# Backward attention loop: the loads of a head put one by one between the DMA transposes, in a fixed order of the SP queue, and the stores moved a few units later

## Chip, cores, metric

One core of a Trainium2 chip. The metric is the device time of one execution in microseconds (us). SP is the engine that issues most DMAs; PE does matmuls, ACT the exponentials, DVE the products, POOL some additions. "Issue" is the time that an engine's sequencer spends on starting a DMA; the transfer itself runs on 16 DMA engines.

## The reference, cut to what matters

The reference is a transformer block (layer norm with modulation, attention with 32 heads of 16, squared-ReLU MLP) and the gradients of its inputs by `jax.vjp`; n = 2048 tokens, D = 512. The part at issue is the gradient of attention:

```
scores = jnp.einsum('bhqd,bhkd->bhqk', q, k) * Dh ** (-0.5)
p = _softmax(scores, axis=-1)
o = jnp.einsum('bhqk,bhkd->bhqd', p, v)
```

From the incoming gradient dO the kernel forms dS = P * (dO v' - row sum) and from it dK, dV and dQ.

## The kernel before

The backward loop handles 4 heads at a time (a "head group", here also just "head"; 8 in all) and in each 64 units of 128 queries x 512 keys. For a unit PE computes the scores and dO v', ACT the exponentials `E_u`, DVE the product `dS_u`, and SP issues a DMA that transposes `dS_u` (128 x 2048 bf16, 512 KB) from SBUF to SBUF, because dQ needs it with keys on the partitions. PE's `dqacc` reads the result 4 units later. PE, ACT and DVE follow the program's order (`manual_schedule`); the order of SP's DMAs is chosen by the recording layer's scheduler.

```python
def load_rows(dst, srcT, hg, cols, aux=None):
    for h in range(4):
        i = hg * 4 + h
        SP.dma_start(out=dst[32 * h:32 * h + DH, :], in_=srcT[i * DH:(i + 1) * DH, cols])            # 16 rows, 64 KB
        if aux is not None:
            SP.dma_start(out=dst[32 * h + DH:32 * h + DH + 1, :], in_=aux[i:i + 1, cols])            # 1 row, 4 KB
# ... (cut)
def load_kvq(hg):
    hs = hsets[hg % 2]                                   # two sets of k, q, v, do, qs
    load_rows(hs["k"], qkT_st[1], hg, slice(0, n))
    load_rows(hs["q"], qkT_st[0], hg, slice(0, n), m_st)
    load_rows(hs["v"], vT_st, hg, slice(0, n))
    ACT.dma_start(out=hs["qs"][:], in_=q_st[hg])
# ... (cut)
def transpose_unit(u):
    hg, kc, qc, qi = units[u]
    if qi == 0:
        dqt[u // 4] = tpool.tile([P, 4, 16, P], BF, name="dsT", tag="dsT")       # 2 buffers
    SP.dma_start(out=dqt[u // 4][:, qi], in_=bst[u][1].rearrange("p h k -> p (h k)"), transpose=True)
# ... (cut)
with tc.manual_schedule(engines={PE.engine, ACT.engine, DVE.engine}):
    for j in range(2 * NU + 10):                         # two steps j for each unit
        # ... load_head of the next head at unit 8; score; dp_pair; transpose_unit; k_quad, v_quad; dq_quad (cut)
```

A head's load is 24 "row loads" (16 of 64 KB for k, q, v and do, 8 of one row) and one load `qs` of 256 KB. At a head's end two results of 512 KB are stored (`dVKtP`, `dQtP`).

## Time and profile before

| | before |
|---|---|
| median, lowest and highest of the first 3 runs | 3083.7 us (3079.6 to 3087.5) |
| backward loop, first to last `dS_u` | 1423.4 to 2891.4 us, 1468.1 us |
| a head (heads 1 to 6) | 182.4 to 184.3 us |
| its 8 blocks of 8 units (head 1) | 25.9, 30.6, 20.6, 22.3, 20.5, 20.8, 21.7, 21.9 us |

The first view is the table by stretches: for the first 25 us of head 1, the next 31 us, and the rest of the head, how long each engine was busy, the granted PE clock, the busy share of the DMA engines and the rate. (Shares above 1 occur as packets overlap.)

```profile
core 0: us, PE busy (x) PEld busy (x) DVE busy (x) ACT busy (x) POOL busy (x), PEclk, DMA share, GB/s
1613.00:1638.00 25.00, 19.48 (x157) 5.06 (x154) 17.66 (x17) 16.82 (x34) 1.38 (x2) 0.78 1.09 218
1638.00:1669.00 31.00, 20.69 (x164) 5.52 (x163) 18.86 (x17) 17.66 (x36) 2.77 (x1) 0.78 0.94 181
1669.00:1797.00 128.00, 113.83 (x963) 32.53 (x960) 111.52 (x97) 104.28 (x208) 13.54 (x11) 0.90 1.16 198
```

In the third stretch everything is busy, DVE 111.52 of 128 us, and DMA over 1. In the second, at the shares of the third PE would have worked 28 us and DVE 27 of the 31; they did 7 to 8 us less, and DMA is below 1.

The next view is SP's timeline at the same place. Columns: start, length, line and operation, destination and source, count; L799 is the transpose, L112 a load of 16 rows, L114 of one row.

```profile
1632.06 1.97 SPq L799 DMA_TRANSPOSE dsT<-dS_u  x1
1634.08 0.99 SPq L112 DMA_DIRECT2D ik_11035<-qkT_st  x1
1635.16 5.70 SPq L799 DMA_TRANSPOSE dsT<-dS_u  x2
1640.91 0.57 SPq L112 DMA_DIRECT2D ik_11035<-qkT_st  x1
1641.53 0.41 SPq L112 DMA_DIRECT2D iq_11037<-qkT_st  x1
1641.99 0.28 SPq L114 DMA_DIRECT2D iq_11037<-m_st  x1
...
1648.73 0.28 SPq L114 DMA_DIRECT2D ido_11038<-d_st  x1
1649.11 8.35 SPq L799 DMA_TRANSPOSE dsT<-dS_u  x3
```

One k load stands alone (1634.08), then two transposes follow, and then 21 loads from 1640.91 to 1649.01, each 0.27 to 0.6 us of issue. For these 8 us SP issues no transpose. DVE's timeline shows the price, in brackets the idle time and who ended it:

```profile
1655.33 1.23 DVE L793 TENSOR_TENSOR dS_u<-psD_u,E_u 128x1024 bf16<-128x1024 f32 x1 [9.53 <-PE psD_u L791]
```

In the middle of a head, SP does nothing but transposes, 13 of them in 34.62 us, 2.66 us each:

```profile
1667.21 34.62 SPq L799 DMA_TRANSPOSE dsT<-dS_u  x13
```

The list of waits (who waited for whom: us in total, times, longest) and the lines of the chain of waits (share of the span):

```profile
DVE dS_u L793 <- PE psD_u L791: 205.8, 122, 10.7
PE dqacc L834 <- DMA dsT<-dS_u: 137.3, 79, 10.5
```

```profile
DMA dsT<-dS_u 14%; ACT ET L569 12%; PE psS_u L779 7%; PE dqacc L834 5%; ACT E_u L781 5%; PE accVK L816 3%; DVE dS_u L793 3%; PE accVK L807 3%; PE psST L567 2%; PE psS_x L779 2%; PE pm L410 2%; DMA dwp<-dw_st 2%; PE pm L430 1%; PE pm L492 1%
```

DVE's longest wait is 10.7 us, a stall like the one above; the entry `DMA dsT<-dS_u 14%` is the largest in the chain.

Which engine sets the pace? I counted the 256 B packets in the trace, 2048 for each transpose. The first packet of a transpose starts on average 0.01 us after the last of the previous one. So the DMA engines go from transpose to transpose without rest, and the loop is the sum of 511 intervals between the ends of neighbouring transposes, sorted here by what SP issued between the two:

```
before: between the transposes    count   interval us (mean)   from last packet to first packet
nothing                            467       2.66 (median 2.50)     0.01
one 64 KB k load                    19       3.38                   0.37
21 row loads                         7      11.01                   8.41
store dVKtP / dQtP                6 / 7      4.15 / 4.21            1.25 / 1.35
```

(Five more intervals, with reloads of gradients for the next stage, are left out here.)

A run of 21 loads costs 11.01 - 2.66 = 8.35 us, three single k loads 3 x 0.72 = 2.2 us: 10.5 us for the row loads of a head, 7 times. (The last of the 7 had only one k load alone, so there are 19 and not 21.)

### The profile page before, as it was taken

Reading aid. Unit: us, or ns where it says so; the run is one execution under the profiler, and the core shown is the slowest. Engines: PE = TensorE matmul, PEld = TensorE weight load, DVE = VectorE, ACT = ScalarE, POOL = GpSimd, SP = SyncE. Lnnn points to the kernel's source line nnn. Section 1 sums busy time; section 2 is a strip of 40 time slices with the busy share of each in tenths; the row PEclk is TensorE's granted clock in tenths of the full one; section 3 lists DMA queues with packets and bytes.
Section 4 is the critical chain, followed back from the end, with each engine's and each line's share of the span. In section 5 each row is a group of like instructions: output and inputs, shape, how many; then the busy total and the mean of one; then the engine's idle time right before and its main releaser. Section 6 shows DMA issues by size and latency. Waiting matters only on the chain.

```text
span 3082.2 us, 46295 instructions
## 1 busy us (share of the span) xinstructions
PE 2460.6 (80%) x17006; PEld 721.4 (23%) x17006; DVE 1785.3 (58%) x2165; ACT 2176.8 (71%) x3415; POOL 519.8 (17%) x487
## 2 busy tenths in 40 slices
PE   6799888688858885546887878878787887988878
PEld 2111122222212221222222222222222222222323
DVE  6000234333423442456787878878787887878783
ACT  4799989698859884103786868778686886877621
POOL 2110012211231224122010110101011010101151
PEclk9555589879986998777788978889798987888888
DMA  9741132724492359677999999999999999999941
GB/s 258 180 130 28 34 69 85 184 59 92 95 152 55 85 112 140 129 151 204 196 197 194 201 193 198 205 191 198 193 201 193 198 205 193 196 211 200 210 112 45
DMA packets 1403811, 475.54 MB, mean 154 GB/s; under 512 B 1321456, under 2 KB 1372660, under 8 KB 1403456
## 3 DMA queue, kind: packets, MB, share of 16 engines
q1 hardware_dynamic: 1390048, 445.31, 74.4%
q0 software_dynamic: 12384, 25.17, 5.0%
q8 instruction: 134, 2.20, 0.3%
q10 hardware_dynamic: 1152, 2.10, 0.3%
q14 instruction: 93, 0.76, 0.1%
HBM read 74.86 MB, written 70.54 MB: 47 GB/s over the span
## 4 chain that ended last, share of the span: by engine, by line
PE 32%; DMA 21%; ACT 17%; issue 11%; DVE 9%; SPq 3%; POOL 3%; DVEq 0%; POOLq 0%; ACTq 0%
DMA dsT<-dS_u 14%; ACT ET L569 12%; PE psS_u L779 7%; PE dqacc L834 5%; ACT E_u L781 5%; PE accVK L816 3%; DVE dS_u L793 3%; PE accVK L807 3%; PE psST L567 2%; PE psS_x L779 2%; PE pm L410 2%; DMA dwp<-dw_st 2%; PE pm L430 1%; PE pm L492 1%; DMA dw_st<-dwp 1%
## 5 line engine op out<-in xcount | busy, mean ns | idle before, releaser
L793 DVE TENSOR_TENSOR dS_u<-psD_u,E_u 128x1024 bf16<-128x1024 f32 x1024 | 1188.2, 1218 | 283.5 <-PE psD_u L791 205.8
L781 ACT ACTIVATE E_u<-psS_u 128x512 bf16<-128x512 f32 x1536 | 867.5, 635 | 316.0 <-PE psD_u L791 304.2
L569 ACT ACTIVATE ET<-psST 128x1024 bf16<-128x1024 f32 x1024 | 952.3, 1249 | 158.7 <-PE psST L567 157.9
L834 PE MATMUL dqacc<-dsT,KS_tok 128*32 128x512 bf16 x2048 | 210.9, 499 | 194.6 <-DMA dsT<-dS_u 137.3
L781 ACT ACTIVATE E_u<-psS_x 128x512 bf16<-128x512 f32 x512 | 334.8, 654 | 10.2 <-PE psD_u L791 9.3
L779 PE MATMUL psS_u<-ik_11035,iq_11037 32*128 32x512 bf16 x768 | 260.2, 435 | 8.8 <-DVE prows L712 3.4
L779 PE MATMUL psS_u<-ik_12082,iq_12084 32*128 32x512 bf16 x768 | 255.0, 425 | 3.9
L583 PE MATMUL oacc<-ET,vaug 128*32 128x512 bf16 x2048 | 253.8, 486 | 1.3 <-DVE ostage L587 1.3
L791 PE MATMUL psD_u<-iv_11036,ido_11038 32*128 32x512 bf16 x1024 | 225.2, 433 | 14.1 <-DVE dS_u L793 10.8
L849 POOL TENSOR_TENSOR dQacc<-dQacc,dqtmp 128x512 f32<-128x512 f32 x64 | 81.1, 1267 | 895.2 <-ACT dqtmp L844 895.2
L567 PE MATMUL psST<-qt_sb_107,kt_sb_105 32*128 32x512 bf16 x1024 | 203.4, 480 | 33.6 <-ACT ET L569 10.9
L791 PE MATMUL psD_u<-iv_12083,ido_12085 32*128 32x512 bf16 x1024 | 219.4, 422 | 6.7 <-DVE dS_u L793 3.9
L816 PE MATMUL accVK<-E_u,dOs_tok 128*16 128x512 bf16 x2048 | 224.6, 428 | 0.0
L567 PE MATMUL psST<-qt_sb_108,kt_sb_106 32*128 32x512 bf16 x1024 | 195.1, 477 | 27.1 <-ACT ET L569 14.3
L338 DVE COPY dwp<-pm 128x512 f32<-128x512 f32 (+1 forms) x102 | 67.3, 660 | 229.7 <-DMA dw_st<-dwp 152.3
L587 DVE COPY ostage<-oacc 128x512 f32<-128x512 f32 x32 | 22.0, 686 | 260.5 <-PE oacc L583 260.5
L331 PE MATMUL pm<-tk,h_c 128*128 128x512 bf16 (+1 forms) x256 | 70.7, 408 | 81.8 <-DVE dwp L338 67.7
L807 PE MATMUL accVK<-dS_u,qz_12075 128*32 128x512 bf16 x1024 | 113.6, 433 | 8.8 <-ACT vkb L819 6.2
L807 PE MATMUL accVK<-dS_u,qz_12076 128*32 128x512 bf16 x1024 | 109.7, 416 | 8.0 <-ACT vkb L819 7.0
L834 PEld LDWEIGHTS <-KS_tok 128*32 128x32 bf16 x2048 | 52.0, 105 | 254.4 <-issue 220.6
L779 PE MATMUL psS_x<-ik_11035,iq_11037 32*128 32x512 bf16 x256 | 106.1, 415 | 0.4
L779 PE MATMUL psS_x<-ik_12082,iq_12084 32*128 32x512 bf16 x256 | 101.9, 398 | 0.3
(747 smaller groups left out, 2559.3 us busy)
## 6 DMA issues: line engine op xcount, KB each, us to landing
dw_st<-dwp POOLq DMA_DIRECT2D x90, 256.0 KB, 4.3
dsT<-dS_u SPq DMA_TRANSPOSE x512
dwp<-dw_st SPq DMA_DIRECT2D x30, 256.0 KB
wA<-in_B_w_dram SPq DMA_DIRECT2D x4, 1792.0 KB
wB<-in_B_w_dram SPq DMA_DIRECT2D x4, 1792.0 KB
qkT_st<-qkT SPq DMA_DIRECT2D x4, 1024.0 KB
kt_sb_105<-qkT_st SPq DMA_DIRECT2D x64, 64.0 KB
kt_sb_106<-qkT_st SPq DMA_DIRECT2D x64, 64.0 KB
```

Source lines behind the costliest of these rows:

```text
L331: PE.matmul(acc[:, 0:w], ops[ti][0], ops[ti][1], start=(ti == 0), stop=(ti == 3))
L567: PE.matmul(ps[:, hi, :], kt_sb[r:r + 32, kt * P:(kt + 1) * P], qt_sb[r:r + 32, :], start=True, stop=True, tile_position=(r, 0))
L569: ACT.activation(ET[:, 2 * pair:2 * pair + 2, :], ps[:], AF.Exp, scale=SCALE)
L583: PE.matmul(oacc[32 * hq:32 * hq + 32, :], lhsT, ET[:, hq, :], start=(kt == 0), stop=(kt == TT - 1), tile_position=(0, 32 * hq), skip_grou ...
L779: PE.matmul(psS[:], st["q"][r:r + 32, qt * P:(qt + 1) * P], st["k"][r:r + 32, kc * 512:kc * 512 + 512], start=True, stop=True, tile_positi ...
L781: ACT.activation(bst[u][0][:, hq, :], psS[:], AF.Exp, scale=SCALE)
L791: PE.matmul(psD[:, hi, :], st["do"][r:r + 32, qt * P:(qt + 1) * P], st["v"][r:r + 32, kc * 512:kc * 512 + 512], start=True, stop=True, til ...
L793: DVE.tensor_tensor(dS_u[:, 2 * pair:2 * pair + 2, :], psD[:], E_u[:, 2 * pair:2 * pair + 2, :], ALU.mult)
L807: PE.matmul(cur["vk"][32 * hq:32 * hq + 32, :], hst[hg]["qz"][:, qt, hq, :], bst[u][1][:, hq, :], start=(qt == 0), stop=False, tile_positi ...
L816: PE.matmul(acc[32 * hq:32 * hq + DH, :], dOs_tok[:, qt, (hg * 4 + hq) * DH:(hg * 4 + hq + 1) * DH], E_u[:, hq, :], start=False, stop=(qt ...
L834: PE.matmul(acc[32 * hq:32 * hq + 32, :], KS_tok[:, kc * 4 + kt, h * DH:h * DH + 32], tT[:, :, hq * 4 + kt, :], start=(kt == 0), stop=(kt ...
L849: POOL.tensor_tensor(dst2, dst, tmp[:], ALU.add)
```

## The change

Its intent: no burst of loads. SP's order becomes fixed like that of the other engines, and the 25 loads of a head go one at a time after every second transpose, through the head before; `qs` moves from ACT's queue to SP's; the two stores are issued 4 and 6 steps later, so that SP doesn't wait for them. Four reloads of gradients in the last head, for the next stage, are spread in the same way. Cut to its core:

```diff
-        def load_kvq(hg):
+        def kvq_loads(hg):
             hs = hsets[hg % 2]
-            load_rows(hs["k"], qkT_st[1], hg, slice(0, n))
-            load_rows(hs["q"], qkT_st[0], hg, slice(0, n), m_st)
-            load_rows(hs["v"], vT_st, hg, slice(0, n))
-            ACT.dma_start(out=hs["qs"][:], in_=q_st[hg])
+            yield hs["qs"][:], q_st[hg]
+            yield from row_loads(hs["k"], qkT_st[1], hg, slice(0, n))
+            yield from row_loads(hs["q"], qkT_st[0], hg, slice(0, n), m_st)
+            yield from row_loads(hs["v"], vT_st, hg, slice(0, n))
 ...
+        def dma(to, fro):
+            SP.dma_start(out=to, in_=fro)
 ...
+        def plan_head(hg):
+            j0 = (hg - 1) * 128 + 14
+            loads = list(kvq_loads(hg)) + list(row_loads(hsets[hg % 2]["do"], dOT_st, hg, slice(0, n), d_st))
+            for i, (to, fro) in enumerate(loads):
+                at(j0 + 4 * i, dma, to, fro)
+            at(j0 + 40, spread_qz, hg)
 ...
-                        SP.dma_start(out=dVKtP[hg], in_=hst[hg]["vk"][:])
+                        at(cur["j"] + 4, dma, dVKtP[hg], hst[hg]["vk"][:])
 ...
-                        SP.dma_start(out=dQtP[hg], in_=st["dq"][:])
+                        at(cur["j"] + 6, dma, dQtP[hg], st["dq"][:])
 ...
-        with tc.manual_schedule(engines={PE.engine, ACT.engine, DVE.engine}):
+        with tc.manual_schedule(engines={PE.engine, ACT.engine, DVE.engine, SP.engine}):
 ...
+                for f, args in todo.pop(j, ()):
+                    f(*args)
```

(`at(j, f, ...)` files a call for step j.)

More of the change, by code (lines that the diff above doesn't have):

```diff
@@ L106, with row_loads, load_rows @@
     gb_bc = modbc[:, 5, :]
-    def load_rows(dst, srcT, hg, cols, aux=None):
+    def row_loads(dst, srcT, hg, cols, aux=None):
         for h in range(4):
             i = hg * 4 + h
-            SP.dma_start(out=dst[32 * h:32 * h + DH, :], in_=srcT[i * DH:(i + 1) * DH, cols])
+            yield dst[32 * h:32 * h + DH, :], srcT[i * DH:(i + 1) * DH, cols]
             if aux is not None:
-                SP.dma_start(out=dst[32 * h + DH:32 * h + DH + 1, :], in_=aux[i:i + 1, cols])
+                yield dst[32 * h + DH:32 * h + DH + 1, :], aux[i:i + 1, cols]
+    def load_rows(*args):
+        for to, fro in row_loads(*args):
+            SP.dma_start(out=to, in_=fro)
     vaugpool = tc.alloc_tile_pool(name="vaugp", bufs=1, side="right")
@@ L682, in head_set @@
             hsets.append(hs)
-        def load_kvq(hg):
+        def kvq_loads(hg):
             hs = hsets[hg % 2]
-            load_rows(hs["k"], qkT_st[1], hg, slice(0, n))
-            load_rows(hs["q"], qkT_st[0], hg, slice(0, n), m_st)
-            load_rows(hs["v"], vT_st, hg, slice(0, n))
-            ACT.dma_start(out=hs["qs"][:], in_=q_st[hg])
+            yield hs["qs"][:], q_st[hg]
+            yield from row_loads(hs["k"], qkT_st[1], hg, slice(0, n))
+            yield from row_loads(hs["q"], qkT_st[0], hg, slice(0, n), m_st)
+            yield from row_loads(hs["v"], vT_st, hg, slice(0, n))
         head_set(0)
-        load_kvq(0)
+        for to, fro in kvq_loads(0):
+            SP.dma_start(out=to, in_=fro)
         with ExitStack() as ph2:
@@ L735, with load_grads @@
     xs = {}
-    def load_grads(hg, tiles):
-        for key, dsrc, xt in (("dq", dQtP, tiles[0]), ("vk", dVKtP, tiles[1])):
-            if (hg, key) not in xs:
+    def load_grads(hg, tiles, which=None):
+        for i, (key, dsrc, xt) in enumerate((("dq", dQtP, tiles[0]), ("vk", dVKtP, tiles[1]))):
+            if (hg, key) not in xs and which in (None, i):
                 xs[hg, key] = xt
@@ L755, in load_head @@
             st = dict(hsets[hg % 2])
-            if hg > 0:
-                load_kvq(hg)
-            load_rows(st["do"], dOT_st, hg, slice(0, n), d_st)
             st["qz"] = qz[hg % 2]
-            POOL.tensor_scalar(qz[hg % 2][:, :, :, DH:2 * DH], st["qs"].rearrange("p t (h d) -> p t h d", h=4),
-                               SCALE, None, ALU.mult)
             st["acc"] = stg.tile([P, n], F32, name="dQacc", tag="dQacc", bufs=1)
@@ L765, in load_head, with at, spread_qz @@
             hst[hg] = st
+        todo = {}
+        def at(j, f, *args):
+            todo.setdefault(j, []).append((f, args))
+        def dma(to, fro):
+            SP.dma_start(out=to, in_=fro)
+        def spread_qz(hg):
+            st = hsets[hg % 2]
+            POOL.tensor_scalar(qz[hg % 2][:, :, :, DH:2 * DH], st["qs"].rearrange("p t (h d) -> p t h d", h=4),
+                               SCALE, None, ALU.mult)
+        def plan_head(hg):
[4 more added lines that the diff above has]
+            at(j0 + 40, spread_qz, hg)
         def score(u, hq, shared):
@@ L853, in dq_quad @@
                     else:
-                        SP.dma_start(out=dQtP[hg], in_=st["dq"][:])
+                        at(cur["j"] + 6, dma, dQtP[hg], st["dq"][:])
+        load_rows(hsets[0]["do"], dOT_st, 0, slice(0, n), d_st)
+        spread_qz(0)
         load_head(0)
+        for hg in range(1, HG):
+            plan_head(hg)
+        for i, key in enumerate(("q", "k", "v", "do")):
+            at((HG - 1) * 128 + 14 + 8 * i, load_grads, i // 2, (hsets[0]["q"], hsets[0]["k"]) if i < 2 else (hsets[0]["v"], hsets[0]["do"]), i % 2)
         SP.dma_start(out=wT_pad[:], in_=wT_st.rearrange("j p d -> p j d"))
-        with tc.manual_schedule(engines={PE.engine, ACT.engine, DVE.engine}):
+        with tc.manual_schedule(engines={PE.engine, ACT.engine, DVE.engine, SP.engine}):
             for j in range(2 * NU + 10):
                 u, pair, sub = j // 2, j % 2, j % 8
+                cur["j"] = j
                 if j < 2 * NU:
@@ L863 @@
                         load_head(units[u][0] + 1)
-                    if pair == 0 and units[u] == (HG - 1, 2, 0, 0):
-                        load_grads(0, (hsets[0]["q"], hsets[0]["k"]))
-                        load_grads(1, (hsets[0]["v"], hsets[0]["do"]))
                     for hi in range(2):
@@ L878 @@
                         dq_quad(b, kt)
+                for f, args in todo.pop(j, ()):
+                    f(*args)
+            assert not todo
     qpool.release()
```

## The prediction

> **What bounds the kernel now.** The change touches only the backward loop, 1423 to 2901 us of 3082. In the table by stretches, between head boundaries (1669 to 1797 us) PE is busy 89%, DVE 87%, ACT 81%, and the DMA share is above 1. Counting 256 B packets (2048 for each of 512 transposes of dS_u), the first packet of a transpose starts on average 0.01 us after the last of the one before: the stream never rests. Ends of neighbouring transposes with nothing between are 2.66 us apart (median 2.50). So the loop is bound by DMA: 512 such intervals plus what is put between transposes.
>
> **What is between them before.** By DVE's dS_u products, heads 1 to 6 take 182.5 to 184.3 us. Most blocks of 8 units take about 21.2 us, the first two of a head 25 and 30: 13.4 us too much. The intervals account for it: a run of 21 small loads, issued by SP at 0.3 to 0.5 us each, makes one interval 11.0 us (8.35 over); three single k loads, 3.38 each (0.7 over); two 512 KB stores, 4.15 and 4.2 (1.5 over). In the run the DMA engines are half idle, waiting for SP's issues. There are 7 such runs.
>
> **What the change does.** No byte is removed. A head's 24 row loads and its q load (moved from ACT's queue) go one after every second transpose of the head before; stores come a few units later. Other engines' work is the same. SP can issue a load while a transpose drains (unhindered it issues in 1.3 to 1.8 us, and drains in 2.5). So the issue-bound part disappears; engine time stays. The Trainium skill ("DMA: Bandwidth & Descriptors", Issuing engines are not separate DMA queues) says all queues share the 16 engines. The trace agrees with sharing: the run's 216 packets of 4096 B (13x16 + 8x1, so a one-row load uses one engine) take 0.22 us each, and no transpose packets fill in.
>
> **Sum per head.** Row loads before: 8.35 + 3 x 0.72 = 10.5 us. After, estimated from the single loads: 16 of 64 KB at 0.45 (0.23 of packets, the rest a bubble as the next transpose is issued later; single loads cost 0.4 to 0.5 at the head's end, 1.1 after the stores), 8 one-row loads at 0.25: 9.2 us. The q load (about 1 us) and stores (3) are paid in both. Gain 1.3 us a head, 9 us in seven, give or take 25: if loads cost only their packets it is 35; at 0.7 each it is a loss of some 25. The large visible stall disappears; its cost comes back in small pieces.
>
> **Prediction.** 3073 us, 3042 to 3100 in 8 of 10. Faster by over 2%: 0.06; within 2%: 0.90; slower by over 2%: 0.04.
>
> **What would show it.** A head's first two blocks fall from 25 and 30 us to about 22; the others rise from 21.2 to 22 or 22.5; heads take 180 to 184 us. The 9 us waits of PE and DVE disappear; PE's waits in dqacc for dsT grow. Intervals with nothing between stay 2.5 to 2.7; with a 64 KB load, 3.0 to 3.2; with a one-row load, about 2.9; stores still cost 1.5. Other stages: unchanged.
>
> **What would make it wrong.** If loads slip into a transpose's drain for nothing (intervals under 2.8), the gain is up to 50 us. If each switch from transpose to copy and back drains the queue, or the lagged issues hold SP ahead of a ready transpose, it is slower. If compute, not DMA, paces the blocks, mid-head loads are free and the gain nears 75 us.

## The result

| | before | after |
|---|---|---|
| median of 4 runs | 3082.4 us (3079.6 to 3087.5) | 3101.8 us (3094.0 to 3103.0) |
| ratio | | 1.0056, 95% interval 1.0034 to 1.0077 |
| first to last `dS_u` | 1468.1 us | 1485.4 us |
| heads 1 to 6 | 182.4 to 184.3 us | 184.5 to 186.5 us |
| blocks of head 1 | 25.9, 30.6, 20.6, 22.3, 20.5, 20.8, 21.7, 21.9 | 23.8, 24.9, 22.9, 23.2, 23.6, 22.1, 22.6, 23.1 |

The change is within 2%, but it makes the kernel slower, by 0.3 to 0.8%. The granted clock doesn't explain it: it was 0.799 to 0.812 in these four runs, and 0.801 to 0.812 in those of the first experiment below, which are 47 us faster.

The table by stretches for the same head of the changed kernel:

```profile
core 0: us, PE busy (x) PEld busy (x) DVE busy (x) ACT busy (x) POOL busy (x), PEclk, DMA share, GB/s
1618.00:1642.00 24.00, 19.78 (x165) 5.25 (x162) 18.87 (x17) 17.94 (x37) 1.72 (x2) 0.78 1.10 204
1642.00:1667.00 25.00, 20.18 (x167) 5.16 (x164) 18.79 (x17) 17.60 (x35) 2.77 (x1) 0.78 1.06 208
1667.00:1804.00 137.00, 116.29 (x960) 31.67 (x956) 111.47 (x97) 104.45 (x207) 13.25 (x11) 0.85 1.09 191
```

The first two blocks are better (49 us for the first two stretches, 56 before), as intended. The third stretch now takes 137 us for the same number of DVE instructions (x97) that took 128; the DMA share fell from 1.16 to 1.09. SP's timeline in the middle of this head (L820 the transpose, L774 every other DMA):

```profile
1703.19 0.67 SPq L774 DMA_DIRECT2D iq_11037<-m_st  x1
1703.96 5.34 SPq L820 DMA_TRANSPOSE dsT<-dS_u  x2
1709.35 0.86 SPq L774 DMA_DIRECT2D iq_11037<-qkT_st  x1
1710.30 4.50 SPq L820 DMA_TRANSPOSE dsT<-dS_u  x2
1714.85 0.73 SPq L774 DMA_DIRECT2D iq_11037<-m_st  x1
1715.68 4.57 SPq L820 DMA_TRANSPOSE dsT<-dS_u  x2
1720.30 0.82 SPq L774 DMA_DIRECT2D iv_11036<-vT_st  x1
```

SP never rests: a pair of transposes, a load of 0.67 to 0.86 us, a pair of transposes. In the run of before most loads of the same size took 0.27 to 0.31 us once the run was under way (the first ones 0.57 and 0.41, and the k load alone behind a transpose 0.99). Nor does SP wait for data, though its list of waits names `dS_u`:

```profile
SPq L820 <- DVE dS_u L814: 916.5, 468, 6.7
```

That can't be what held it: in heads 1 to 6 `dS_u` was done 2.8 us (median) before SP began to issue its transpose, and after a load never less than 0.75 us before. The waits and the chain:

```profile
DVE dS_u L814 <- PE psD_u L812: 208.8, 139, 3.8
PE dqacc L855 <- DMA dsT<-dS_u: 177.5, 105, 4.5
```

```profile
DMA dsT<-dS_u 18%; ACT ET L573 11%; PE psS_u L800 7%; PE dqacc L855 6%; ACT E_u L802 5%; DVE dS_u L814 3%; PE accVK L837 3%; PE accVK L828 2%; PE psST L571 2%; PE pm L414 2%; PE psS_x L800 2%; PE pm L496 1%; PE pm L434 1%; DMA dwp<-dw_st 1%
```

The 10 us stall of DVE is gone (longest wait 3.8), but its total is the same (205.8 then, 208.8 now), PE waits 177.5 us for transposes instead of 137.3, and the transposes have 18% of the chain instead of 14%. The intervals, counted as before:

```
after: between the transposes     count   interval us (mean)   from last packet to first packet
nothing                            318       2.64 (median 2.52)     0.00
one 64 KB load (k, q, v, do)       112       3.26                   0.45
one row (m, d)                      56       3.01                   0.25
q load 256 KB                        7       3.62                   1.05
store dVKtP / dQtP                6 / 7      4.14 / 4.07            1.40 / 1.27
```

For the row loads of a head that is 16 x (3.26 - 2.64) + 8 x (3.01 - 2.64) = 12.9 us, against 10.5 before: 2.4 us more in 7 heads, 17 us. The loop is 17.3 us longer. (Two terms are left out that cancel: the q load, new on SP's queue, adds 1 us a head, 7 in all; the mean interval with nothing between, in which its packets fell before, is 0.015 us shorter, 7 us over 467.) So the place of the loss is settled by the two traces; why a load costs so much more than its packets is not.

### The profile page after: what moved, and what is told of

It reads as the page before. It is cut to its first block, busy times and chain, and to the rows that moved or that the text cites. A ratio compares the mean times of both kernels' runs of the same rounds, so it can differ in the third digit from the quotient of the medians.

```text
span 3101.2 us, 46431 instructions
## 1 busy us (share of the span) xinstructions
PE 2479.1 (80%) x17006; PEld 720.3 (23%) x17006; DVE 1789.1 (58%) x2165; ACT 2177.2 (70%) x3415; POOL 519.8 (17%) x487
## 4 chain that ended last, share of the span: by engine, by line
PE 31%; DMA 24%; ACT 17%; issue 11%; DVE 10%; POOL 2%; SPq 2%; DVEq 0%; POOLq 0%; ACTq 0%
DMA dsT<-dS_u 18%; ACT ET L573 11%; PE psS_u L800 7%; PE dqacc L855 6%; ACT E_u L802 5%; DVE dS_u L814 3%; PE accVK L837 3%; PE accVK L828 2%; PE psST L571 2%; PE pm L414 2%; PE psS_x L800 2%; PE pm L496 1%; PE pm L434 1%; DMA dwp<-dw_st 1%; PE oacc L587 1%
## 5 line engine op out<-in xcount | busy, mean ns | idle before, releaser
L814 DVE TENSOR_TENSOR dS_u<-psD_u,E_u 128x1024 bf16<-128x1024 f32 x1024 | 1192.0, 1217 | 297.1 <-PE psD_u L812 208.8
L855 PE MATMUL dqacc<-dsT,KS_tok 128*32 128x512 bf16 x2048 | 222.8, 524 | 196.9 <-DMA dsT<-dS_u 177.5
L812 PE MATMUL psD_u<-iv_11036,ido_11038 32*128 32x512 bf16 x1024 | 224.7, 432 | 15.7 <-DVE dS_u L814 13.4
L812 PE MATMUL psD_u<-iv_12083,ido_12085 32*128 32x512 bf16 x1024 | 227.4, 438 | 4.7 <-DVE dS_u L814 3.1
```

The costliest lines, as they stand in the source:

```text
L812: PE.matmul(psD[:, hi, :], st["do"][r:r + 32, qt * P:(qt + 1) * P], st["v"][r:r + 32, kc * 512:kc * 512 + 512], start=True, stop=True, til ...
L814: DVE.tensor_tensor(dS_u[:, 2 * pair:2 * pair + 2, :], psD[:], E_u[:, 2 * pair:2 * pair + 2, :], ALU.mult)
L855: PE.matmul(acc[32 * hq:32 * hq + 32, :], KS_tok[:, kc * 4 + kt, h * DH:h * DH + 32], tT[:, :, hq * 4 + kt, :], start=(kt == 0), stop=(kt ...
```

## The experiments

Theory A: SP. It runs only a little ahead of the DMA engines, and a load that it has to issue between two transposes makes the next transpose late. Rival B: the DMA engines. They change from transpose to copy and wait for HBM, or the load's bytes stand in the transposes' own queue; who issues it is all one. Rival C: the fixed order or the later stores cost it, not the loads.

### The loads on ACT's queue (e1_act_queue)

```diff
+        def dma_load(to, fro):
+            ACT.dma_start(out=to, in_=fro)
-                at(j0 + 4 * i, dma, to, fro)
+                at(j0 + 4 * i, dma_load, to, fro)
```

> The spread loads of the changed kernel, at the same places, but issued by ACT on its own queue. Theory A (a load between two transposes costs 0.6 us, of which 0.23 are its packets and the rest is SP issuing the next transpose later): SP issues transposes alone, a load then costs its packets only, 0.2 us; 24 x 0.3 us x 7 heads = 50 us less than the changed kernel, about 3050 us, intervals with a load 2.8 to 2.9 us. Theory B (the cost is in the DMA engines: they change from transpose to copy and wait for the read from HBM, whoever issues it): 3095 to 3105 us, intervals still 3.0 to 3.3 us.

Measured: 3054.8 us, ratio to before 0.9909 (0.9892 to 0.9926); correct. It beats both kernels: 28 us under before, 47 under the change by the medians (45 by the ratios). SP, in the same stretch of time as above:

```profile
1699.07 33.24 SPq L823 DMA_TRANSPOSE dsT<-dS_u  x12
```

Twelve transposes in 33.24 us, 2.77 each, and nothing between them. ACT puts a load between two exponentials:

```profile
1701.66 1.12 ACT L805 ACTIVATE E_u<-psS_u 128x512 bf16<-128x512 f32 x2
1702.26 0.31 ACTq L777 DMA_DIRECT2D iv<-vT_st  x1
1702.61 0.66 ACT L805 ACTIVATE E_u<-psS_x 128x512 bf16<-128x512 f32 x1
...
1706.67 0.31 ACTq L777 DMA_DIRECT2D iv<-vT_st  x1
1706.99 1.86 ACT L805 ACTIVATE E_u<-psS_u 128x512 bf16<-128x512 f32 x3
```

The issue takes 0.31 us and delays nothing: the exponentials go on at 1702.61 and 1706.99 without idle time noted. PE's wait for transposes falls below that of the kernel before:

```profile
PE dqacc L858 <- DMA dsT<-dS_u: 111.7, 70, 4.6
```

Its intervals, each load put to that transpose in whose interval its packets must fall, are 2.98 us with a 64 KB load and 2.66 us with one row, against 2.66 with nothing: a 64 KB load now costs about 0.3 us, near its packets (0.22), and a row little. (How a row load is assigned matters: by its packet's own end the row comes to 2.82, the 64 KB load to 3.00, nothing to 2.64.) A holds, and a pure B falls: same loads, same places, same 16 engines. But the load has also left the transposes' queue, which the next run separates.

### The same with a dose of SP issue (e8_act_plus_tiny)

Loads on ACT as above, and at each of the 175 places SP also issues a load of 32 bytes into a tile that nothing reads:

```diff
+                at(j0 + 4 * i, dma_load, to, fro)
+                at(j0 + 4 * i, dma, tinyt[0:1, 16 * i:16 * i + 16], m_st[i:i + 1, 0:16])
```

> The run with the loads on ACT's queue, and at each of the 175 places SP also issues a load of 32 bytes into an unused tile, as dose of issue time without data. If the loss of the spread loads is SP's issue (one issue holds the next transpose back by 0.25 to 0.35 us, whatever it moves), 175 x 0.3 = 50 us come back: about 3100 us, intervals with a tiny load 0.3 us longer than those without. If the loss was the bytes standing in the same queue as the transposes, the tiny loads cost nothing: 3050 to 3060 us.

Measured: 3092.5 us, ratio 1.0035 (1.0022 to 1.0049); correct. So 38 of the 47 us that separate the two kernels come back with 175 issues that move 5.6 KB in all: 0.22 us each, somewhat under the 0.3 expected. (In the two profiled executions the loop's transposes take 1474.9 us against 1427.7, 0.27 each.) SP's timeline:

```profile
1702.36 0.42 SPq L774 DMA_DIRECT2D tinyt<-m_st  x1
1702.88 4.47 SPq L826 DMA_TRANSPOSE dsT<-dS_u  x2
1707.40 0.66 SPq L774 DMA_DIRECT2D tinyt<-m_st  x1
1708.15 5.05 SPq L826 DMA_TRANSPOSE dsT<-dS_u  x2
```

A load of 32 bytes takes 0.42 to 0.66 us of SP. The issue is most of the cost, not the bytes; the remaining 9 us may be the longer issues of the real loads (0.67 to 0.85 us on average, 0.57 for the tiny ones) or their bytes in the same queue; this is not separated.

The mechanism can be read off by three durations for each transpose, averaged over heads 1 to 6: how long before the last packet of the previous transpose SP had finished issuing that one ("lead"), how long until SP began to issue the next, and how long from there to its first packet:

```
us                           lead    to the next issue    issue to first packet    idle engines
after, nothing between       1.77          0.10                  1.66                  0.00
after, 64 KB load            1.72          0.98                  1.18                  0.44
after, one row               1.78          0.81                  1.22                  0.25
tiny load on SP              1.70          0.72                  1.25                  0.27
before, single k load        1.86          1.03                  1.19                  0.37
```

The last column is the sum of the middle two less the lead. A transpose needs about 1.2 us from its issue to its first packet, and SP's lead is 1.7 us, so SP has half a microsecond to spare at each transpose. Any other DMA takes 0.7 to 1.0 us with the gaps around it. (With nothing between, the third column is longer as the packets queue behind the previous transpose.) The third column also answers a rival that the tiny loads leave: that the queue loses time by changing from a copy to a transpose. The shortest issue to first packet is 1.17 us after a load and 1.17 us with nothing between, in the five traces checked, so no such time is seen. Two things stay open. One is why the lead stays at 1.7 us: with nothing between, SP spends 2.6 us on a transpose's issue, after a load 2.1 to 2.2, though 1.3 us occurs, and no run shows what holds it. The other is why a load's issue takes longer behind a transpose than in a run of loads.

### All loads at one place again (e4_one_run)

```diff
-                at(j0 + 4 * i, dma, to, fro)
+                at(j0, dma, to, fro)
```

> The changed kernel with all 25 loads of a head at one place (after the 7th transpose of the head before), fixed order and lagged stores kept. If spreading is what costs, and fixed order and stores cost nothing, this is the kernel before again: 25 x 0.4 = 10 us a head, 3080 us (3074 to 3088), one interval of about 12.5 us a head. If fixed order or the later stores are what costs, it stays near 3100 us.

Measured: 3084.0 us, ratio 1.0010 (0.9995 to 1.0024); correct. The interval with 25 loads is 13.4 us (12.5 expected). This is the time of the kernel before with the fixed order and the later stores kept, so rival C falls: these two parts of the change together cost and gain nothing that can be seen, and the loss belongs to the spreading.

### Groups of four (e3_groups_of_4)

```diff
-                at(j0 + 4 * i, dma, to, fro)
+                at(j0 + 16 * (i // 4), dma, to, fro)
```

> The same loads on SP's queue, four at once after every eighth transpose. If there is a fixed cost for each interruption of the transpose stream (about 0.3 us) and about 0.3 us for each load, a group of 4 costs about 1.5 us and the kernel falls to about 3080 us. If the cost is SP's issue time alone beyond what a drain hides, a group of 4 costs 4 x 0.45 - 0.6 = 1.2 us (with its packets at least 0.9), about 3070 us. If each load costs the same wherever it stands (0.53 us on average), 3101 us.

Measured: 3084.1 us, ratio 1.0007 (0.9992 to 1.0021); correct. A group costs 4.45 - 2.65 = 1.8 us, 0.45 a load, nearest to the first expectation (1.5 us, 3080 us); alone a row load costs 0.54 on average, in the run of 25 it is (13.40 - 2.66) / 25 = 0.43. (Without the group that holds the q load, a group costs 4.29 - 2.65, 0.41 a load.) So a load that stands alone has a price of its own, about 0.1 us, which four together already avoid; on SP's queue spreading won at neither dose.

### No row loads (e5_no_loads)

```diff
-                at(j0 + 4 * i, dma, to, fro)
+                if i == 0:
+                    at(j0 + 4 * i, dma, to, fro)
```

> Wrong results on purpose: the changed kernel without the 24 row loads of heads 1 to 7 (the q load stays). If the loads cost what their intervals show (16 x 0.62 + 8 x 0.38 = 12.9 us a head), 3101 - 90 = 3011 us (3003 to 3020). If part of an interval's length would pass anyway because compute sets the pace, the gain is smaller: 3040 us or more.

Measured: 3017.9 us, ratio 0.9798 (0.9781 to 0.9814); wrong results, as intended. The row loads cost 84 us in the changed kernel, 12.0 a head, near the 12.9 that the intervals gave: nearly all of an interval's length is real time. They cost 64 us in the kernel before (the intervals gave 72) and 37 us on ACT's queue (5.3 a head, 0.33 for each of the 16 loads of 64 KB). SP's timeline has 12 transposes in 32.13 us:

```profile
1699.51 32.13 SPq L821 DMA_TRANSPOSE dsT<-dS_u  x12
```

### One run on ACT's queue (e6_one_run_act)

```diff
+            ACT.dma_start(out=to, in_=fro)     # as dma_load
-                at(j0 + 4 * i, dma, to, fro)
+                at(j0, dma_load, to, fro)
```

> All 25 loads of a head at one place again, but issued by ACT. If the queue alone matters, and spreading doesn't, it is as fast as the spread loads on ACT, 3050 to 3060 us. But ACT is then held for 25 x 0.3 = 8 us in one piece, while it is busy 81% of the time: exponentials come late and transposes dry up for some 2 to 4 us a head, so I expect 3065 to 3080 us. 3083 us or more if spreading is what makes ACT's queue work at all.

Measured: 3112.1 us, ratio 1.0097 (1.0081 to 1.0113); correct. Slower than all others: the expectation was missed by 30 us. ACT's timeline:

```profile
1631.77 0.34 ACTq L777 DMA_DIRECT2D iqs<-q_st  x1
1632.15 0.47 ACTq L777 DMA_DIRECT2D ik<-qkT_st  x1
1632.66 4.58 ACTq L777 DMA_DIRECT2D ik<-qkT_st  x3
1640.66 0.31 ACTq L777 DMA_DIRECT2D iq<-qkT_st  x1
...
1650.32 0.29 ACTq L777 DMA_DIRECT2D ido<-d_st  x1
1650.66 1.08 ACT L805 ACTIVATE E_u<-psS_u 128x512 bf16<-128x512 f32 x2 [17.84 <-DMA ido<-dOT_st]
```

ACT is held from 1631.77 to 1650.61, 19 us and not 8, with empty stretches between issues (one ends at 1640.66). The trace's operands say why: DMAs of SP and ACT use eight semaphores in turn, and each load here waits for the DMA that had its semaphore before, eight places back, to land. Twenty-five loads in a row run into transposes that are still to land, and the exponentials behind them, on which the next transposes depend, wait too. So ACT's queue needs the spreading that SP's queue can't bear. The trace also has the size: of the 19 us, 9.9 are the 25 issues themselves, and four gaps between them, 8.2 us in all, each end about 0.02 us after the landing that the next load waits for (1640.64 for the load at 1640.66). Over the 7 heads ACT is held 21 us on average, 11 of them in gaps.

### POOL's queue (e2_pool_queue)

As the first experiment with `POOL.dma_start`, and POOL too in fixed order.

> The loads issued by POOL, which is idle most of the loop (busy about 10% in it), on its own queue, in order with its additions, so in clumps of 8 and then 2 per block. If freeing SP is what gains, 3045 to 3062 us, as with ACT. If ACT's queue gained for another reason (hardware queue with few packets), POOL's software queue gives 3080 us or more.

Measured: 3069.1 us, ratio 0.9965 (0.9949 to 0.9981); correct; the profiled run was the slowest of its six, 3079.2 us. It is faster than before, which again needs no SP issue, but not as fast as ACT, so the expected range was missed. POOL has nothing to wait for in the first half of a head, so its order holds the loads back only by its own additions: in the trace 9 of a head's 25 come within 6 to 7 us and the rest in pairs, much as expected. The interval in which most of the 9 fall is 6.3 to 9.4 us long (heads 1 to 6), and the first block of heads 1 to 6 takes 26 to 30 us where ACT's took 21 to 25. Whether POOL's queue is itself dearer is open.

### Stores on ACT's queue too (e7_stores_act_too)

```diff
-                        at(cur["j"] + 4, dma, dVKtP[hg], hst[hg]["vk"][:])
+                        at(cur["j"] + 4, dma_load, dVKtP[hg], hst[hg]["vk"][:])
```

(and so for `dQtP`)

> As the run with the loads on ACT's queue, the 13 stores of 512 KB go there too. An interval with a store is 1.5 us longer, and the store's own packets take 8 x 0.22 = 1.8 us on each engine: so the bytes are the cost and the queue doesn't matter, 3055 us plus or minus 5. If SP's issue is part of it (0.3 us each), 13 x 0.3 = 4 us less, which these rounds hardly show.

Measured: 3052.3 us, ratio 0.9909 (0.9891 to 0.9927), the same as the loads alone; correct. Who issues a store makes no difference that these rounds can show, which fits the expectation that its bytes are its cost.

## Why the prediction was right and wrong

- Right: the change lies within 2%, the DMA engines bound the loop, the large stall disappears "and its cost comes back in small pieces". Blocks evened out (25.9 and 30.6 us became 23.8 and 24.9 in head 1, the rest rose to about 23), PE's waits for `dsT` grew, intervals with nothing between stayed at 2.64 us, stores still cost 1.5. That the class was right says little: every correct run here lies within 1% of the kernel before.
- Wrong: the sign and the size. A gain of 9 us was forecast, a loss of 19 measured; the median lies 2 us above the range's end.
- The step that failed: "SP can issue a load while a transpose drains (unhindered it issues in 1.3 to 1.8 us, and drains in 2.5). So the issue-bound part disappears". It compared SP's issue time with the drain, 1.3 to 1.8 plus a load's 0.3 to 0.5 against 2.5, and left out the way from issue to first packet. (Its own sum took some of this back, with a bubble of about 0.2 us for each load; measured it is 0.44.) SP can't start the next transpose late and make it up: 1.2 us must pass from its issue, and SP's lead is only 1.7 us. Behind a transpose a load also holds SP not 0.3 but 0.7 to 0.85 us. The run with loads on ACT shows the size of what did not disappear, 47 us, and the tiny loads bring 38 of it back.
- The terms of the sum that this mis-sized: a 64 KB load at 0.45, measured 0.62; a one-row load at 0.25, measured 0.37. With these the sum is 12.9 us a head in place of 9.2, and 7 x (12.9 - 10.5) = 17 us. The trace of before had single k loads at 0.72, and I discounted them as disturbed by the stores near by. It held the mechanism too: these k loads, 16 in heads 1 to 6, kept SP 0.88 us each and left the engines idle for 0.37 us (last row of the table above).
- The condition "at 0.7 each it is a loss of some 25" comes near what came: 0.62, and a loss of 19.
- That "the lagged issues hold SP ahead of a ready transpose" stood among the reasons to be wrong, without a size. It needed no wait for data: `dS_u` was done at least 0.75 us before each issue that followed a load, and the listed waits of SP's loads and stores in the loop are 4.2 us in all.

## What to carry to other kernels

What these runs suggest: before spreading small DMAs through a stream of large ones, find out how far the issuing queue runs ahead of the DMA engines and how long a transfer takes from its issue to its first packet; only the difference is free, and each extra issue is set against it, whatever its bytes. If it doesn't fit, give the small DMAs to another engine's queue, spread thinly if that engine has work of its own: here ACT's queue with spreading gains 0.9%, SP's with spreading loses 0.6%, and ACT's without it loses 1.0%. A burst that looks like a stall of 9 us may be the cheapest form on its own queue.

## What the Trainium skill lacked or had wrong

- "DMA: Bandwidth & Descriptors", Issuing engines are not separate DMA queues, says that issuing on several engines "will only save the time on the sequencer it takes to initiate the DMA, which is usually small relative to the DMA itself". What it saves is confirmed, that it is small is not: a 64 KB load took 0.22 us of each engine's time and 0.8 us of SP's, and moving 175 loads to ACT saved 47 us of 3102. The page doesn't say that a DMA's issue behind a transpose takes longer than alone (0.8 us against 0.3 for the same 16 rows, 0.7 against 0.27 for one row).
- The same page, Latency and other measured facts, gives about 600 ns to the first byte of a DMA issued by SP or ACT. A transpose here took 1.2 us from the start of its issue on SP to its first packet when the engines were idle; the section has no such figure for transposes. The figure for a plain load was not tested here.
- The same section gives 261 GB/s for a DMA transpose "with non-contiguous mid-dim", measured on one kernel, and about 350 to 400 for the contiguous case. Here 512 KB from SBUF to SBUF in packets of 256 B drained in 2.50 us (median), which is 210 GB/s, below both.
- No page has the eight semaphores that the recording layer shares between DMAs of SP and ACT, nor that a run of DMAs on a compute engine's queue is thereby held: 25 issues took 19 us in one head, 8.2 of them in gaps that ended with the landing of the DMA eight places before.
